# Decay products over 128 tokens instead of 64 in an attention that feeds two matrix layers

## The chip, the core and the metric

The kernel runs on one core of a Trainium2 chip. That core has a matrix engine (TensorE, PE in the profile; its weight loads are PEld), a vector engine (VectorE, DVE), a scalar engine (ScalarE, ACT), a third elementwise engine (GpSimd, POOL) and a queue that issues transfers (SyncE, SP). The metric is the device time of one execution in microseconds.

## What is computed

A recurrent attention over 4 batches, 8 heads and 768 tokens of width 48, and behind it two layers of 384 to 2048 to 384 over the 3072 tokens. Per head, token by token:

```
cur   = (u * k_t) outer v_t
y_t   = r_t @ (state + cur)
state = w_t[:, None] * state + k_t outer v_t
```

The first layer has the activation 0 below -1, h above 1 and (h+1)^2/4 between; the second has h * sigmoid(1.702 h). Weights come as 64-bit floats and are turned into 32-bit floats on the chip; every 32-bit product is made of three products of rounded parts (high by high, high by low, low by high).

## The kernel before

**Windows.** The attention is done in 24 windows of 128 tokens of one batch, 6 per batch, all 8 heads at once: 4 head pairs `m`, two heads `hh` of a pair on partitions 0 to 63 and 64 to 127. A window has two chunks `c` of 64 tokens, so 8 pieces `mc`. Inside a window the decays are products: two scans on VectorE (L423 from the right end of a piece, L425 from the left) make `rr` and `pp`, both in one buffer `pi`; k is multiplied by `rr` (L430, VectorE), r by `pp` (GpSimd). In the first seven windows (`RIP_N = 7`) r is scaled in place (L433) and ScalarE copies it into the two tiles `ra` later (L484); from the eighth on GpSimd writes the scaled r straight into `ra`, with two instructions of 64 partitions (L437). Each piece has a slot of 65 elements in `pi`, and a product starts anew in each.

**Scores and state.** The matrix engine transposes k (L464), makes the scores `sc` of each piece (L469) and the products k by v of both chunks, `kv` (L498). A tile `ra` holds scaled r in one half of the partitions and masked scores in the other (L474 copies them in under a mask, after L455 has put the u term on the diagonal). A tile `lt` holds the state in one half and v in the other, so that one matmul with K = 128 gives y (L504, `yt`). The state of the first chunk is put into `lt` by GpSimd, multiplied by the chunk's whole product `pcs` (`put`, L446); after `kv` VectorE adds it to the state (`upd`, L510) into `us`, GpSimd multiplies `us` by the second chunk's product and puts it in the second chunk's place of `lt` (L446 again), and `yt` of the second chunk follows. ScalarE squares all scaled values with a running sum (L449, L450, L486, L528): the sums decide at the end whether the numbers stayed in range.

**Layers.** The 3072 tokens go through each layer in 8 tiles of 384, in 16 steps a tile. A step `s` is: nine matmuls into `hp` (L651; two buffers while the attention runs), the low part `gl` of step s-1 (L676), nine matmuls of step s-3 into `acc` (L660, second layer L669), and the activation of step s: DVE L688, ACT L689, DVE L701, ACT L682 for the high part `gh`. A buffer of `hp` is free when L701 has read it, two steps on.

**Order.** Up to step 15 of the first tile a scheduler orders the instructions, with its own model of durations. In that part the 32 pieces of the first layer's weights are converted (DVE L638 and L642, ACT L640, POOL L644) and split (L169, L178). From step 16 on every engine's order is the order of the code. Three windows are spread over the 16 steps of a tile: a window is a generator that does one portion per slot (`attn_slot`), and 24 slots fall on 16 steps, so that windows meet the steps in three different positions, which come back in every tile. The second layer's weights are converted in the same stretch (ACT L640, L147, L148 and the vector engines).

Of the kernel before, what the change touches and what calls it, by code (L numbers as in the profile page):

```python
# [9 lines left out]
F32 = mybir.dt.float32  # L10
# [3 lines left out]
AF = mybir.ActivationFunctionType  # L14
ALU = mybir.AluOpType
# [86 lines left out]
def fast_path(st, tc, rkw_t, nat, v_l, w1, w2, u, out, x2_d, w2_d, flag_i, force):  # L102
# [79 lines left out]
    def eng_of(pat, i):  # L182
        return (nc.gpsimd, nc.vector)[pat[i % len(pat)]]
# [156 lines left out]
    with ExitStack() as sa:  # L340
# [9 lines left out]
        stu = at.tile([128, 2], F32, name="stu")  # L350
        stat = at.tile([128, NW, 4], F32, name="stat")
        rk = [at.tile([128, RKW], F32, name=f"rk{i}") for i in range(2)]
        lt = [at.tile([128, 2, MC * D + 16], F32, name=f"lt{i}") for i in range(2)]

        def slots(t, a, j):
            return t[:, a:a + WW].rearrange("p (a b) -> p a b", b=C + 1)[:, :, j]

        def consts():
            nc.gpsimd.memset(ident, 1.0)
            nc.gpsimd.affine_select(out=ident, in_=ident, pattern=[[-1, 128]], compare_op=ALU.is_equal, fill=0.0, base=0, channel_multiplier=1)  # L360
            nc.scalar.activation(out=idn, in_=ident, func=AF.Copy, scale=-1.0)
            nc.gpsimd.memset(mk_f, 1.0)
            for hh in range(2):
                p = slice(64 * hh, 64 * hh + 64)
                nc.gpsimd.affine_select(out=mk_f[p], in_=mk_f[p], pattern=[[1, C]], compare_op=ALU.is_gt, fill=0.0, base=0, channel_multiplier=-1)
            nc.vector.tensor_copy(mask, mk_f)
            nc.vector.memset(one_s, PMIN)
            nc.vector.memset(slots(one_s, 1, C), 1.0)
            nc.vector.memset(seed, PMIN)

        def prep(i):
# [20 lines left out]
        def load_v(n):  # L392
            i = n % 2
            tv = a2.tile([128, NP, 2, D], F32, tag="vn", name="vn")
            nc.sync.dma_start(out=tv, in_=nat[n, :, 2 * MC * D:].rearrange("p (m h d) -> p m h d", h=2, d=D))
            vn_t[n] = tv
            for hh in range(2):
                p = slice(64 * (1 - hh), 64 * (1 - hh) + 64)
                nc.sync.dma_start(out=lt[i][p, hh, 0:MC * D], in_=v_l[n, hh])

        tile_of = {}
        for i, (t0, n) in enumerate(TILES):
# [3 lines left out]
        def window(n):  # L406
# [10 lines left out]
            pi = a2.tile([128, 2 * WW + 1], F32, tag="pi", name="pi", bufs=PI_B)  # L417
            pp, rr = pi[:, 0:WW], pi[:, WW:]
            pcs = a2.tile([128, MC], F32, tag="pcs", name="pcs")
# [18 lines left out]
            def lt_s(t, hh, c):  # L438
                p = slice(64 * hh, 64 * hh + D)
                return t[p, hh, 0:MC * D].rearrange("p (m c d) -> p m c d", c=NC2, d=D)[:, :, c, :]  # L440

            def put(us, c):
                for hh in range(2):
                    p = slice(64 * hh, 64 * hh + D)
                    pc = pcs.rearrange("p (m c) -> p m c", c=NC2)[p, :, c:c + 1].to_broadcast([D, NP, D])
                    nc.gpsimd.tensor_tensor(out=lt_s(lt[i], hh, c), in0=us[p], in1=pc, op=ALU.mult)  # L446

            yield
            nc.scalar.activation(out=pp, in_=pp, func=AF.Square, accum_out=stat[:, n, 0:1])  # L449
            nc.scalar.activation(out=rr[:, 1:], in_=rr[:, 1:], func=AF.Square, accum_out=stat[:, n, 3:4])  # L450
            nc.vector.tensor_reduce(bb, nt[:, 0:MC * D].rearrange("p (a d) -> p a d", d=D), axis=AX.X, op=ALU.add)
            yield
            for hh in range(2):
                p = slice(64 * (1 - hh), 64 * (1 - hh) + 64)
                nc.gpsimd.affine_select(out=ra[hh][p], in_=bb[p, :, None].to_broadcast([64, MC, C]), pattern=[[0, MC], [1, C]], compare_op=ALU.is_equal, fill=0.0, base=0, channel_multiplier=-1)  # L455
            if PUT == 0 and not first:
                put(carry.pop(), 0)
            yield
            if n + 1 < NW:
                load_rkn(n + 1)  # L460
# [5 lines left out]
            for mc in range(MC):  # L466
                for hh in range(2):
                    p = slice(64 * hh, 64 * hh + D)
                    nc.tensor.matmul(out=sc[64 * (1 - hh):64 * (1 - hh) + 64, mc, :], lhsT=kt[p, mc, :], rhs=(rt[p, mc, :] if n < RIP_N else ra[hh][p, mc, :]), start=True, stop=True)  # L469
            kn_t = a2.tile([128, NP, 128], F32, tag="ktok", name="ktok", bufs=1)  # L470
            nc.scalar.activation(out=kn_t, in_=tp, func=AF.Copy)
            for hh in range(2):
# [44 lines left out]
            if not last:  # L517
                carry.append(upd(1))
# [296 lines left out]
def layout(inputs):  # L815
    r, k, v, w, u = (inputs[n] for n in "rkvwu")
    res = {}

    def tr(a):
        a = a.reshape(B, NP, 2, WPB, W, D).transpose(0, 3, 2, 5, 1, 4)  # L820
        return a.reshape(NW, 2, D, NP * W)

    wt = np.zeros((NW, 2, D, MC, C + 1), np.float32)
    wt[..., 1:] = tr(w).reshape(NW, 2, D, MC, C)
# [9 lines left out]
    res["v_l"] = nat(v)  # L834
# [29 lines left out]
```

## Time and profile before

| | us |
|---|---|
| median of 3 runs | 1037.53 |
| lowest and highest run | 1035.62, 1037.84 |
| the profiled execution | 1035.07 |
| its span, first to last instruction | 1033.3 |
| PE busy in it | 950.6 (92%) |
| DVE, ACT, POOL busy | 604.1, 517.5, 469.6 |

The page's slices show the matrix engine's busy share below 90% in the first six of 40 slices and at 90% or more in nearly all of the rest. Busy matmuls are pipelined, so a busy matrix engine is not one at its peak; what counts is where it waits.

### The profile page before, as it was taken

How to read it: one execution, taken by the hardware profiler on the slowest of the kernel's cores; microseconds unless marked ns; L12 is line 12 of the kernel's file. 1: busy time of each engine (PE TensorE's matmuls, PEld its weight loads, DVE VectorE, ACT ScalarE, POOL GpSimd, SP SyncE). 2: the span in 40 equal slices, each digit the busy share in tenths (PEclk: the TensorE clock that was granted, in tenths of full speed). 3: DMA queues.
4: the chain of work that ended last, by engine and by line, in shares of the span. 5: the costliest groups of instructions: out<-in, count | busy, mean ns of one | idle time of the engine just before them, and what ended most of it. 6: DMA issues, size and time to landing. Idle time of an engine off the chain costs nothing.

```text
span 1033.3 us, 18712 instructions
## 1 busy us (share of the span) xinstructions
PE 950.6 (92%) x6976; PEld 903.7 (87%) x6976; DVE 604.1 (58%) x1007; ACT 517.5 (50%) x1221; POOL 469.6 (45%) x481
## 2 busy tenths in 40 slices
PE   4645889999999999999999999999999999999997
PEld 2434769989888988898989999999999999999997
DVE  8999984787877777778674663323232323232321
ACT  5654554565555655546653565455555433333332
POOL 6897872676676666766662342111111111111111
PEclk8756989999999999999999999999999999999999
DMA  9763422644534545434310543232323110101000
GB/s 250 203 191 107 129 56 56 188 126 128 145 103 110 147 129 142 131 103 126 101 43 5 167 153 108 62 107 62 108 62 109 30 46 1 47 2 46 15 9 27
DMA packets 52228, 100.20 MB, mean 97 GB/s; under 512 B 8608, under 2 KB 34464, under 8 KB 52128
## 3 DMA queue, kind: packets, MB, share of 16 engines
q1 hardware_dynamic: 52128, 98.91, 33.2%
q8 instruction: 57, 0.93, 0.4%
q14 instruction: 43, 0.35, 0.1%
HBM read 81.97 MB, written 15.73 MB: 95 GB/s over the span
## 4 chain that ended last, share of the span: by engine, by line
PE 57%; DVE 17%; POOL 8%; ACT 6%; issue 6%; DMA 4%; SPq 2%; POOLq 0%; ACTq 0%; DVEq 0%
PE hp L651 27%; PE acc L669 20%; PE acc L660 8%; DVE pi L423 2%; DVE t L701 2%; ACT gh L682 2%; DVE ra L474 2%; DVE pi L425 2%; DVE gl L676 1%; DVE wt L638 1%; DMA wst<-w 1%; POOL ra L437 1%; POOL rkn L426 1%; POOL wt L644 1%; DVE wt L642 1%
## 5 line engine op out<-in xcount | busy, mean ns | idle before, releaser
L676 POOL TENSOR_TENSOR gl<-t,gh 128x384 fp32r<-128x384 f32 x128 | 132.0, 1031 | 387.7 <-ACT gh L682 386.1
L682 ACT ACTIVATE gh<-t 128x384 fp32r<-128x384 f32 x256 | 133.9, 523 | 205.5 <-DVE t L701 122.9
L712 DVE TENSOR_TENSOR t<-t,hp 128x384 f32<-128x384 f32 x128 | 70.8, 553 | 218.6 <-ACT t L707 218.1
L707 ACT ACTIVATE t<-hp 128x384 f32<-128x384 f32 x128 | 63.0, 492 | 145.8 <-PE hp L651 145.8
L660 PE MATMUL acc<-gh,whi 128*128 128x384 f32 x384 | 132.4, 350 | 0.3 <-DVE ev L252 0.3
L660 PE MATMUL acc<-gl,whi 128*128 128x384 f32 x384 | 130.2, 339 | 1.2 <-DVE gl L676 1.2
L669 PE MATMUL acc<-wlo,gh 128*128 128x384 f32 x384 | 130.2, 339 | 0.0
L669 PE MATMUL acc<-whi,gh 128*128 128x384 f32 x384 | 129.9, 338 | 0.0
L660 PE MATMUL acc<-gh,wlo 128*128 128x384 f32 x384 | 129.6, 338 | 0.0
L669 PE MATMUL acc<-whi,gl 128*128 128x384 f32 x384 | 129.3, 337 | 0.0
L651 PE MATMUL hp<-xh,whi 128*128 128x384 f32 x384 | 95.9, 359 | 24.1 <-DVE t L701 23.0
L676 DVE TENSOR_TENSOR gl<-t,gh 128x384 fp32r<-128x384 f32 x128 | 81.4, 636 | 47.0 <-ACT gh L682 44.6
L689 ACT ACTIVATE t<-t 128x384 f32<-128x384 f32 x128 | 66.3, 518 | 78.7 <-DVE t L688 76.8
L701 DVE TENSOR_TENSOR t<-t,hp 128x384 f32<-128x384 f32 x128 | 70.1, 548 | 51.9 <-ACT t L689 51.1
L644 POOL TENSOR_TENSOR wt<-wt,wb 128x384 int32<-128x384 int32 x64 | 71.7, 1121 | 62.0 <-ACT wb L640 51.1
L651 PEld LDWEIGHTS hp<-xh,whi 128*128 128x128 f32 x384 | 67.8, 193 | 33.3 <-DVE t L701 29.9
L688 DVE TENSOR_SCALAR t<-hp 128x384 f32<-128x384 f32 x128 | 70.4, 550 | 41.7 <-PE hp L651 41.6
L651 PE MATMUL hp<-xl,whi 128*128 128x384 f32 x384 | 90.2, 344 | 0.0
L651 PE MATMUL hp<-xh,wlo 128*128 128x384 f32 x384 | 89.4, 341 | 0.0
L651 PE MATMUL hp<-x2l,whi 128*128 128x384 f32 x384 | 88.8, 339 | 0.0
L651 PE MATMUL hp<-x2h,wlo 128*128 128x384 f32 x384 | 88.0, 337 | 0.0
L651 PE MATMUL hp<-x2h,whi 128*128 128x384 f32 x384 | 87.4, 335 | 0.0
(106 smaller groups left out, 1944.3 us busy)
## 6 DMA issues: line engine op xcount, KB each, us to landing
wst<-w SPq DMA_DIRECT2D x96, 384.0 KB, 3.4
rk<-rkw_t SPq DMA_DIRECT2D x48, 289.7 KB, 4.9
rkn<-nat SPq DMA_DIRECT2D x24, 384.0 KB, 4.1
w_d<-wt SPq DMA_DIRECT2D x32, 192.0 KB, 3.3
w2f<-w_d SPq DMA_DIRECT2D x32, 192.0 KB, 2.5
vn<-nat SPq DMA_DIRECT2D x24, 192.0 KB, 3.0
lt<-v_l SPq DMA_DIRECT2D x48, 96.0 KB, 3.0
x_d<-ev SPq DMA_DIRECT2D x24, 192.0 KB, 2.5
```

The source lines that it names most:

```text
L423: nc.vector.tensor_tensor_scan(out=rr[:, WW:0:-1], data0=ws[:, WW:0:-1], data1=one_s[:, WW:0:-1], initial=0.0, op0=ALU.mult, op1=ALU.max)
L644: nc.gpsimd.tensor_tensor(out=t, in0=t, in1=b, op=ALU.add)
L651: nc.tensor.matmul(out=hp[:, 0:n], lhsT=win(a, f, kk), rhs=b[:, kk, 0:n], start=(i == 0), stop=(i == 3 * KD - 1))
L660: nc.tensor.matmul(out=acc[j][:, 0:n], lhsT=wout(a, f, j * 128, 128), rhs=b[:, 0:n], start=(f == 0 and i == 0), stop=(f == KF - 1 and i == 2))
L669: nc.tensor.matmul(out=o[:, 0:DM], lhsT=a[:, j * 128:(j + 1) * 128], rhs=wout(b, f, 0, DM), start=(f == 0 and i == 0), stop=(f == KF - 1 a ...
L676: eng.tensor_tensor(out=gl[:, 0:n], in0=t[:, 0:n], in1=gh[:, 0:n].bitcast(F32), op=ALU.subtract)
L682: nc.scalar.activation(out=gh[:, 0:n], in_=t[:, 0:n], func=AF.Copy)
L688: nc.vector.tensor_scalar(t[:, 0:n], hp[:, 0:n], scalar1=-1.0, scalar2=1.0, op0=ALU.max, op1=ALU.min)
L689: nc.scalar.activation(out=t[:, 0:n], in_=t[:, 0:n], func=AF.Square, bias=0.5, scale=0.5)
L701: nc.vector.tensor_tensor(out=t[:, 0:n], in0=t[:, 0:n], in1=hp[:, 0:n], op=ALU.max)
L707: nc.scalar.activation(out=t[:, 0:n], in_=hp[:, 0:n], func=AF.Sigmoid, scale=1.702)
L712: nc.vector.tensor_tensor(out=t[:, 0:n], in0=t[:, 0:n], in1=hp[:, 0:n], op=ALU.mult)
```

## The change

The products run over a whole window of 128 tokens: 4 slots of 129 elements instead of 8 of 65. Then:

- `pcs` has 4 columns instead of 8 and is copied by ScalarE instead of VectorE.
- r is scaled in place by GpSimd in all windows (one instruction of 128 partitions); ScalarE copies it into both `ra` in all windows.
- The state of the second chunk is the sum alone: VectorE writes it straight into `lt`; GpSimd's second `put` is gone, and the addition stands ahead of the first chunk's `yt` in the code.
- The two halves of `pi` are squared by one instruction; r and k by two instead of one. Scale factors keep the squares in range.
- `lt` has slots of 64 elements instead of 48, filled by a load of 128 KB instead of 96 KB.

```diff
-WW = MC * (C + 1)
+WW = NP * (W + 1)
-PMIN = 1e-10
+PMIN = 1e-15
+DSC = 1e-5
-K_E = (1,)
-RIP_N = 7
-        lt = [at.tile([128, 2, MC * D + 16], F32, name=f"lt{i}") for i in range(2)]
+        lt = [at.tile([128, 2, MC, 64], F32, name=f"lt{i}") for i in range(2)]
...
-            nc.vector.tensor_copy(pcs, slots(rr, 1, 0))
-            eng_of(K_E, n).tensor_tensor(out=kt, in0=kt, in1=rr[:, 1:].rearrange("p (a b) -> p a b", b=C + 1)[:, :, 1:C + 1], op=ALU.mult)
-            pr = pp.rearrange("p (a b) -> p a b", b=C + 1)[:, :, 0:C]
-            if n < RIP_N:
-                nc.gpsimd.tensor_tensor(out=rt, in0=rt, in1=pr, op=ALU.mult)
-            else:
-                for hh in range(2):
-                    p = slice(64 * hh, 64 * hh + 64)
-                    nc.gpsimd.tensor_tensor(out=ra[hh][p], in0=rt[p], in1=pr[p], op=ALU.mult)
+            nc.scalar.activation(out=pcs, in_=slots(rr, 1, 0), func=AF.Copy)
+            kw = rk[i][:, NP * W:OW].rearrange("p (a b) -> p a b", b=W)
+            nc.vector.tensor_tensor(out=kw, in0=kw, in1=rr[:, 1:].rearrange("p (a b) -> p a b", b=W + 1)[:, :, 1:W + 1], op=ALU.mult)
+            rw = rk[i][:, 0:NP * W].rearrange("p (a b) -> p a b", b=W)
+            nc.gpsimd.tensor_tensor(out=rw, in0=rw, in1=pp.rearrange("p (a b) -> p a b", b=W + 1)[:, :, 0:W], op=ALU.mult)
...
-            nc.scalar.activation(out=pp, in_=pp, func=AF.Square, accum_out=stat[:, n, 0:1])
-            nc.scalar.activation(out=rr[:, 1:], in_=rr[:, 1:], func=AF.Square, accum_out=stat[:, n, 3:4])
+            sq = pi.rearrange("p (a b) -> p a b", b=WW + 1)[:, :, 0:WW]
+            nc.scalar.activation(out=sq, in_=sq, func=AF.Square, scale=DSC, accum_out=stat[:, n, 0:1])
...
-            if n < RIP_N:
-                for hh in range(2):
-                    p = slice(64 * hh, 64 * hh + 64)
-                    nc.scalar.activation(out=ra[hh][p], in_=rt[p], func=AF.Copy)
-            sq = rk[i][:, 0:OW]
-            nc.scalar.activation(out=sq, in_=sq, func=AF.Square, accum_out=stat[:, n, 1:2])
+            for hh in range(2):
+                p = slice(64 * hh, 64 * hh + 64)
+                nc.scalar.activation(out=ra[hh][p], in_=rt[p], func=AF.Copy)
+            nc.scalar.activation(out=rw, in_=rw, func=AF.Square, scale=DSC, accum_out=stat[:, n, 1:2])
+            nc.scalar.activation(out=kw, in_=kw, func=AF.Square, accum_out=stat[:, n, 3:4])
...
             def upd(c):
-                us = a2.tile([128, NP, D], F32, tag="us", name="us")
+                us = a2.tile([128, NP, D], F32, tag="us", name="us") if c else None
                 for hh in range(2):
                     p = slice(64 * hh, 64 * hh + D)
-                    nc.vector.tensor_tensor(out=us[p], in0=lt_s(lt[i], hh, c), in1=kv[c][p], op=ALU.add)
+                    nc.vector.tensor_tensor(out=us[p] if c else lt_s(hh, 1), in0=lt_s(hh, c), in1=kv[c][p], op=ALU.add)
                 return us
 
             mm_kv()
+            upd(0)
             mm_y(0)
-            put(upd(0), 1)
```

Three places show how instructions move. The first is ScalarE in the part whose order is the code's, at the thirteenth window: `gh` and `t` belong to the layer's steps, `wb` and `wj` to the conversion of the second layer's weights, `ktok` is the transposed k, `rk` the tile of r, k and w, and `ra` the right-hand side of `yt`. Before:

```order
L689 ACTIVATE t<-t 128x384
L471 ACTIVATE ktok<-tp 128x512
L682 ACTIVATE gh<-t 128x384
L640 ACTIVATE wb<-wst 128x384
L147 ACTIVATE wj,wsum<-wst 128x384
L148 ACTIVATE wj,wmin<-wj 128x384
L486 ACTIVATE rk_160,stat<-rk_160 128x1024
L689 ACTIVATE t<-t 128x384
```

The same place now:

```order
L683 ACTIVATE t<-t 128x384
L466 ACTIVATE ktok<-tp 128x512
L676 ACTIVATE gh<-t 128x384
L634 ACTIVATE wb<-wst 128x384
L146 ACTIVATE wj,wsum<-wst 128x384
L147 ACTIVATE wj,wmin<-wj 128x384
L478 ACTIVATE ra_3072<-rk_160 64x512
L478 ACTIVATE ra_3073<-rk_160 64x512
L479 ACTIVATE rk_160,stat<-rk_160 128x512
L480 ACTIVATE rk_160,stat<-rk_160 128x512
L683 ACTIVATE t<-t 128x384
```

Where one square stood there are two copies and two squares; what is ahead of them is the same. The second place is GpSimd in the same part, around the eleventh window: `lt` is the state's tile, `rkn` the products for the u term. Before:

```order
L446 TENSOR_TENSOR lt_163<-us,pcs 48x4x48 x2
L644 TENSOR_TENSOR wt<-wt,wb 128x384
L676 TENSOR_TENSOR gl<-t,gh 128x384
L446 TENSOR_TENSOR lt_163<-us,pcs 48x4x48 x2
L426 TENSOR_TENSOR rkn<-rkn 128x384
L427 TENSOR_TENSOR rkn<-rkn,u_n 128x384
L437 TENSOR_TENSOR ra_2551<-rk_160,pi 64x512
L437 TENSOR_TENSOR ra_2552<-rk_160,pi 64x512
L676 TENSOR_TENSOR gl<-t,gh 128x384
```

The same place now:

```order
L441 TENSOR_TENSOR lt_163<-us,pcs 48x4x48 x2
L638 TENSOR_TENSOR wt<-wt,wb 128x384
L670 TENSOR_TENSOR gl<-t,gh 128x384
L425 TENSOR_TENSOR rkn<-rkn 128x384
L426 TENSOR_TENSOR rkn<-rkn,u_n 128x384
L432 TENSOR_TENSOR rk_160<-rk_160,pi 128x512
L670 TENSOR_TENSOR gl<-t,gh 128x384
```

Two products of the state and one of the two products of r are gone. The third place is VectorE in the scheduled part, around the last conversion of a weight piece (`wt`): `t` and `hp` are the activation of the layer's steps, `wlo` a weight's low part. Before, the last `wt<-wst,wt`:

```order
L510 TENSOR_TENSOR us<-lt_163,kv_1340 48x192 x2
L423 SCALAR_TENSOR_TENSOR pi<-rk_161,one_s 128x520
L178 TENSOR_TENSOR wlo_0_135<-wt,whi_0_103 128x384
L701 TENSOR_TENSOR t<-t,hp 128x384
L424 RECIPROCAL seed<-pi 128x8
L430 TENSOR_TENSOR rk_161<-rk_161,pi 128x512
L701 TENSOR_TENSOR t<-t,hp 128x384
L638 TENSOR_SCALAR wt<-wst 128x384
L425 SCALAR_TENSOR_TENSOR pi<-rk_161,seed 128x520
L642 SCALAR_TENSOR_TENSOR wt<-wst,wt 128x384
```

Now:

```order
L695 TENSOR_TENSOR t<-t,hp 128x384
L682 TENSOR_SCALAR t<-hp 128x384
L670 TENSOR_TENSOR gl<-t,gh 128x384
L695 TENSOR_TENSOR t<-t,hp 128x384
L531 TENSOR_TENSOR xl<-xr,xh 128x3x128
L632 TENSOR_SCALAR wt<-wst 128x384
L682 TENSOR_SCALAR t<-hp 128x384
L177 TENSOR_TENSOR wlo_0_135<-wt,whi_0_103 128x384
L636 SCALAR_TENSOR_TENSOR wt<-wst,wt 128x384
```

The eighth window's scans stand beside the last conversion before and well ahead of it now. Up to the last conversion VectorE's order holds `t<-hp` of nine steps before and of seven now; up to the sixteenth `t<-hp` it holds the same instructions but for the eight copies of `pcs`.

## Rows read from the trace of the kernel before

**Rows 1.** Stages: us, busy us (instructions) of each engine, PE clock, DMA share, GB/s
```profile
0.00:150.00 150.00, 91.10 (x802) 71.34 (x802) 140.31 (x197) 78.87 (x176) 117.67 (x120) 0.76 0.58 159
150.00:550.00 400.00, 383.61 (x3473) 357.12 (x3473) 295.73 (x515) 225.33 (x561) 258.14 (x270) 1.00 0.41 116
```

**Rows 2.** Waits of PE, 150 to 550 us: total, times, longest
```profile
PE hp L651 <- DVE t L701: 10.7, 17, 1.2
PE yt L504 <- POOL lt L446: 3.0, 6, 0.8
PE yt L504 <- POOL lt L477: 2.3, 4, 0.7
```

**Rows 3.** PE in order of time: start, us, instructions, idle before and its releaser
```profile
386.44 0.69 PE L504 MATMUL yt<-ra,lt 128*64 128x64 f32 x16
...
395.00 0.80 PE L651 MATMUL hp<-xh,whi 128*128 128x384 f32 x3 [0.53 <-DVE t L701]
...
398.92 0.80 PE L651 MATMUL hp<-xh,whi 128*128 128x384 f32 x3 [0.49 <-DVE t L701]
...
409.31 0.69 PE L504 MATMUL yt<-ra,lt 128*64 128x64 f32 x16
...
427.74 0.80 PE L651 MATMUL hp<-xh,whi 128*128 128x384 f32 x3 [0.67 <-DVE t L701]
...
430.80 0.33 PE L504 MATMUL yt<-ra,lt 128*64 128x64 f32 x2 [0.71 <-POOL lt L477]
431.55 0.68 PE L504 MATMUL yt<-ra,lt 128*64 128x64 f32 x14 [0.42 <-POOL lt L477]
```

**Rows 4.** ACT in order of time, same stretch
```profile
386.09 1.04 ACT L486 ACTIVATE rk<-rk 128x1024 f32<-128x1024 f32 x1
...
409.31 1.05 ACT L486 ACTIVATE rk<-rk 128x1024 f32<-128x1024 f32 x1
...
422.88 0.64 ACT L449 ACTIVATE pi<-pi 128x520 f32<-128x520 f32 x1 [2.64 <-POOL ra L437]
...
432.97 1.05 ACT L486 ACTIVATE rk<-rk 128x1024 f32<-128x1024 f32 x1
```

**Rows 5.** Groups, whole run: busy us, mean ns, idle before and releasers
```profile
L446 POOL TENSOR_TENSOR lt<-us,pcs 48x192 f32<-48x192 f32 x88 | 52.7, 599 | 18.4 <-DVE us L510 11.1 <-PE yt L504 4.1
L437 POOL TENSOR_TENSOR ra<-rk,pi 64x512 f32<-64x512 f32 x34 | 45.1, 1325 | 14.8 <-DVE pi L425 13.5
L486 ACT ACTIVATE rk<-rk 128x1024 f32<-128x1024 f32 x24 | 25.1, 1044 | 0.1
L449 ACT ACTIVATE pi<-pi 128x520 f32<-128x520 f32 x24 | 15.1, 629 | 10.2 <-POOL ra L437 9.8 <-POOL rk L433 0.3
L433 POOL TENSOR_TENSOR rk<-rk,pi 128x512 f32<-128x512 f32 x7 | 9.2, 1311 | 3.1 <-issue 1.5 <-DVE pi L425 1.4
L484 ACT ACTIVATE ra<-rk 64x512 f32<-64x512 f32 x14 | 8.7, 623 | 0.8 <-POOL rk L433 0.7
L486 ACT ACTIVATION_READ_ACCUMULATOR rk<-rk 128x1 f32 x24 | 4.5, 186 | 0.0
```

**Rows 6.** DVE in order of time, same stretch as rows 3
```profile
390.30 0.36 DVE L510 TENSOR_TENSOR us<-lt,kv 48x192 f32<-48x192 f32 x1 [0.24 <-POOL lt L446]
...
396.65 1.15 DVE L429 COPY pcs<-pi 128x8 f32<-128x8 f32 x1
```

**Rows 7.** Groups of DVE, 0 to 150 us
```profile
L642 DVE SCALAR_TENSOR_TENSOR wt<-wst,wt 128x384 int32<-128x384 int32 x32 | 30.2, 947 | 0.4
...
L429 DVE COPY pcs<-pi 128x8 f32<-128x8 f32 x8 | 5.1, 632 | 0.1
```

**Rows 8.** Line L642 alone, 0 to 150 us: min/median/max ns, first and last start
```profile
L642 DVE SCALAR_TENSOR_TENSOR wt<-wst,wt x32: 525/875/2651, 8.6 to 146.9; 128x384 int32<-128x384 int32 x32
```

**Rows 9.** The last conversion (DVE) and the start of PE's seventeenth step
```profile
146.88 0.53 DVE L642 SCALAR_TENSOR_TENSOR wt<-wst,wt 128x384 int32<-128x384 int32 x1
...
171.56 0.79 PE L651 MATMUL hp<-xh,whi 128*128 128x384 f32 x3
```

More of the change, by code (lines that the diff above doesn't have):

```diff
@@ L367, in consts @@
             nc.vector.memset(one_s, PMIN)
-            nc.vector.memset(slots(one_s, 1, C), 1.0)
+            nc.vector.memset(slots(one_s, 1, W), 1.0)
             nc.vector.memset(seed, PMIN)
@@ L398, in load_v @@
                 p = slice(64 * (1 - hh), 64 * (1 - hh) + 64)
-                nc.sync.dma_start(out=lt[i][p, hh, 0:MC * D], in_=v_l[n, hh])
+                nc.sync.dma_start(out=lt[i][p, hh], in_=v_l[n, hh])
         tile_of = {}
@@ L416, in window @@
             kn = nt[:, MC * D:2 * MC * D].rearrange("p (m c d) -> p m c d", c=NC2, d=D)
-            pi = a2.tile([128, 2 * WW + 1], F32, tag="pi", name="pi", bufs=PI_B)
-            pp, rr = pi[:, 0:WW], pi[:, WW:]
-            pcs = a2.tile([128, MC], F32, tag="pcs", name="pcs")
+            pi = a2.tile([128, 2 * WW + 2], F32, tag="pi", name="pi", bufs=PI_B)
+            pp, rr = pi[:, 0:WW], pi[:, WW:2 * WW + 1]
+            pcs = a2.tile([128, NP], F32, tag="pcs", name="pcs")
             ra = [a2.tile([128, MC, C], F32, tag=f"ra{h}", name=f"ra{h}", bufs=2) for h in range(2)]
@@ L428, in window, with lt_s, put @@
             yield
-            nc.vector.tensor_copy(pcs, slots(rr, 1, 0))
-            eng_of(K_E, n).tensor_tensor(out=kt, in0=kt, in1=rr[:, 1:].rearrange("p (a b) -> p a b", b=C + 1)[:, :, 1:C + 1], op=ALU.mult)
-            pr = pp.rearrange("p (a b) -> p a b", b=C + 1)[:, :, 0:C]
-            if n < RIP_N:
-                nc.gpsimd.tensor_tensor(out=rt, in0=rt, in1=pr, op=ALU.mult)
-            else:
-                for hh in range(2):
-                    p = slice(64 * hh, 64 * hh + 64)
-                    nc.gpsimd.tensor_tensor(out=ra[hh][p], in0=rt[p], in1=pr[p], op=ALU.mult)
-            def lt_s(t, hh, c):
+            nc.scalar.activation(out=pcs, in_=slots(rr, 1, 0), func=AF.Copy)
[3 more added lines that the diff above has]
+            nc.gpsimd.tensor_tensor(out=rw, in0=rw, in1=pp.rearrange("p (a b) -> p a b", b=W + 1)[:, :, 0:W], op=ALU.mult)
+            def lt_s(hh, c):
                 p = slice(64 * hh, 64 * hh + D)
-                return t[p, hh, 0:MC * D].rearrange("p (m c d) -> p m c d", c=NC2, d=D)[:, :, c, :]
-            def put(us, c):
+                return lt[i][p, hh].rearrange("p (m c) e -> p m c e", c=NC2)[:, :, c, 0:D]
+            def put(us):
                 for hh in range(2):
                     p = slice(64 * hh, 64 * hh + D)
-                    pc = pcs.rearrange("p (m c) -> p m c", c=NC2)[p, :, c:c + 1].to_broadcast([D, NP, D])
-                    nc.gpsimd.tensor_tensor(out=lt_s(lt[i], hh, c), in0=us[p], in1=pc, op=ALU.mult)
+                    nc.gpsimd.tensor_tensor(out=lt_s(hh, 0), in0=us[p], in1=pcs[p, :, None].to_broadcast([D, NP, D]), op=ALU.mult)
             yield
-            nc.scalar.activation(out=pp, in_=pp, func=AF.Square, accum_out=stat[:, n, 0:1])
-            nc.scalar.activation(out=rr[:, 1:], in_=rr[:, 1:], func=AF.Square, accum_out=stat[:, n, 3:4])
+            sq = pi.rearrange("p (a b) -> p a b", b=WW + 1)[:, :, 0:WW]
+            nc.scalar.activation(out=sq, in_=sq, func=AF.Square, scale=DSC, accum_out=stat[:, n, 0:1])
             nc.vector.tensor_reduce(bb, nt[:, 0:MC * D].rearrange("p (a d) -> p a d", d=D), axis=AX.X, op=ALU.add)
@@ L456, in window @@
             if PUT == 0 and not first:
-                put(carry.pop(), 0)
+                put(carry.pop())
             yield
@@ L468, in window @@
                     p = slice(64 * hh, 64 * hh + D)
-                    nc.tensor.matmul(out=sc[64 * (1 - hh):64 * (1 - hh) + 64, mc, :], lhsT=kt[p, mc, :], rhs=(rt[p, mc, :] if n < RIP_N else ra[hh][p, mc, :]), start=True, stop=True)
+                    nc.tensor.matmul(out=sc[64 * (1 - hh):64 * (1 - hh) + 64, mc, :], lhsT=kt[p, mc, :], rhs=rt[p, mc, :], start=True, stop=True)
             kn_t = a2.tile([128, NP, 128], F32, tag="ktok", name="ktok", bufs=1)
@@ L490, in window @@
             if PUT == 2 and not first:
-                put(carry.pop(), 0)
+                put(carry.pop())
             yt = ps_s.tile([128, NP, W], F32, tag="s", name="yt")
@@ L503, in mm_y @@
                         mc = m * NC2 + c
-                        nc.tensor.matmul(out=yt[64 * hh:64 * hh + 64, m, c * C:(c + 1) * C], lhsT=lt[i][:, hh, mc * D:mc * D + 64], rhs=ra[hh][:, mc, :], start=True, stop=True)
+                        nc.tensor.matmul(out=yt[64 * hh:64 * hh + 64, m, c * C:(c + 1) * C], lhsT=lt[i][:, hh, mc, :], rhs=ra[hh][:, mc, :], start=True, stop=True)
             def upd(c):
-                us = a2.tile([128, NP, D], F32, tag="us", name="us")
+                us = a2.tile([128, NP, D], F32, tag="us", name="us") if c else None
                 for hh in range(2):
                     p = slice(64 * hh, 64 * hh + D)
-                    nc.vector.tensor_tensor(out=us[p], in0=lt_s(lt[i], hh, c), in1=kv[c][p], op=ALU.add)
+                    nc.vector.tensor_tensor(out=us[p] if c else lt_s(hh, 1), in0=lt_s(hh, c), in1=kv[c][p], op=ALU.add)
                 return us
             mm_kv()
+            upd(0)
             mm_y(0)
-            put(upd(0), 1)
             yield
@@ L821, in tr @@
         return a.reshape(NW, 2, D, NP * W)
-    wt = np.zeros((NW, 2, D, MC, C + 1), np.float32)
-    wt[..., 1:] = tr(w).reshape(NW, 2, D, MC, C)
+    wt = np.zeros((NW, 2, D, NP, W + 1), np.float32)
+    wt[..., 1:] = tr(w).reshape(NW, 2, D, NP, W)
     res["rkw_t"] = np.concatenate([tr(r), tr(k), wt.reshape(NW, 2, D, -1), wt[..., 0, 0:1]], axis=3)
@@ L833, in layout @@
     res["nat"] = np.concatenate([flip(r), flip(k), tok(v)], axis=2)
-    res["v_l"] = nat(v)
+    vl = np.zeros((NW, 2, C, MC, 64), np.float32)
+    vl[..., 0:D] = nat(v).reshape(NW, 2, C, MC, D)
+    res["v_l"] = vl
     def slices(wi, wo):
```

6 lines of the change are left out of this document (3 added, 3 removed).

## The prediction

> **What bounds the kernel now.** I read the stages first. Up to 150 us VectorE is busy 140.31 of 150 us and the matrix engine 91.10: there VectorE sets the pace, and the reader is to see that nearly every microsecond taken from it could come back. From 150 to 550 us the matrix engine is busy 383.61 of 400 us at full clock, so that at most 16.4 us are to be had there, and a new wait on it costs its whole length; the other engines have a quarter or more of that stretch free [rows 1]. After 550 us the attention is over and no instruction of the change is left. Second, the waits of the matrix engine in the middle stage: 10.7 us for a free `hp` buffer (VectorE's L701 is late) and 3.0 + 2.3 us of `yt` for GpSimd's work on `lt` [rows 2]. Third, one tile in order of time, 386 to 432 us, with its three windows, one in each of the three positions that come back in every tile: what stands on ScalarE and VectorE where `yt` starts [rows 3, 4, 6]. Last, durations by group [rows 5, 7].
>
> **Part by part, middle stage.** 17 windows lie in it whose r went to `ra` by GpSimd before and goes through ScalarE now: six like the first of the tile shown, six like the second, five like the third.
>
> GpSimd loses, per window, two products of the state at 599 ns and one r product (2 x 1325 before, 1311 now): 2.5 us [rows 5]. It is busy 258 of 400 us and is no bound [rows 1]; what counts is who waits for it. VectorE loses the copy of `pcs`, 1.15 us in the tile shown [rows 6]. ScalarE's copy of it is not in the trace; it lies between a read-out of one column, 186 ns, and a 64-row copy of 512 columns, 623 ns [rows 5]; I take 0.2 us, near the read-out, since it has 4 columns.
>
> ScalarE gains the two copies, 2 x 623 = 1.25 us, and one read-out; two squares of half the length for one of 1044 ns are between 0.2 and 0.4 us more; one square of `pi` instead of two saves about 2 x (629 + 186) - (1044 + 186) = 0.4 us [rows 5]. Some 1.5 us more in a window, which its free time holds. But the copies are now in the path: `yt` reads `ra`, and the copies stand in ScalarE's queue where L486 stood, behind `ktok` and, in the third position, also behind a weight's `wb` and two `wj`. So I compare the time of L486 with the start of `yt`:
>
> First position: L486 at 386.09, `yt` at 386.44 [rows 3, 4]. The second copy ends at 386.09 + 1.25 = 387.34, so `yt` is 0.9 us late. Nothing upstream is quicker: the square's place there follows work that comes out of a transfer. Six times 0.9 is +5.4.
>
> Second position: L486 and `yt` both at 409.31, so 1.25 us late as it stands. But ScalarE comes there earlier. VectorE no longer waits for GpSimd before its scans (0.24 us, and as much before the instruction ahead of it) and has no `pcs` copy (1.15) [rows 6]; the square of `pi` saves 0.4 and the `pcs` copy on ScalarE takes back 0.2: together about 1.8 us. The same 1.8 us remove the matrix engine's stalls of 0.53 and 0.49 us for `hp` ahead of it [rows 3]. Copies ready at 409.31 - 1.8 + 1.25 = 408.76; `yt` could go at 409.31 - 1.02 = 408.29: 0.47 late, 1.02 gained, net -0.55. Six times is -3.3.
>
> Third position: `yt` could have gone at 430.80 - 0.71 = 430.09 and waited for GpSimd until 431.55 [rows 3]. L486 is at 432.97, so copies as it stands are ready at 434.22. Upstream the square of `pi` at 422.88 had waited 2.64 us for GpSimd's r product [rows 4]; that is 2 x 1.325 - 1.311 = 1.34 us shorter, and the joint square gives 0.4: ready at about 432.5, and the stall of 0.67 us at 427.74 goes meanwhile. What counts is the end: 432.5 against 431.55, +0.95. Five times is +4.8. GpSimd's wait is not saved there, it ends behind a longer one.
>
> Sum: 5.4 - 3.3 + 4.8 = +6.9 us. Bounds: if the copies come in time everywhere, all waits of rows 2 go, -16.0; if ScalarE is no earlier anywhere and nothing is given back, 6 x 0.9 + 6 x 1.25 + 5 x (434.22 - 431.55) = +26.3.
>
> **First stage.** Eight copies of `pcs` leave VectorE, 8 x 632 ns = 5.1 us [rows 7]. About 14 products of the state leave GpSimd, 14 x 599 ns = 8.4 us [rows 5] of the 117.67 it is busy there [rows 1]. VectorE is slowed while GpSimd works: the 32 L642 take 525 ns at least, 947 on average and 2651 at most, 13.5 us over the least [rows 7, 8]. If that falls with GpSimd's work, 8.4/117.67 of it is 1.0 us, and as much again for other instructions: -5 to -7 us of VectorE's work.
>
> The Trainium skill ("SBUF — State Buffer", section "SBUF: two separate sides") says that VectorE and GpSimd lock a shared port pair for a whole instruction and the loser blocks. The spread of L642 agrees; by that rule GpSimd's full 8.4 us could come back, 13 us in all, and that is the faster rival below.
>
> What the matrix engine gets of it depends on the order. Up to the last conversion VectorE's order holds `t<-hp` of seven steps now and of nine before: the conversions end earlier, but two more steps of the matrix engine come behind them. A step takes 398.92 - 0.49 - 395.00 = 3.4 us [rows 3], two 6.9. Before, the seventeenth step starts 171.56 - 146.88 = 24.7 us behind the last conversion [rows 9]. VectorE's instructions up to the last conversion are fewer now by the copies and by two steps' activation (about 4 instructions of some 0.5 us): 5 to 9 us earlier, and 6.9 later behind it. The start of the seventeenth step so moves by -2 +- 5; I take -2, since the work that VectorE loses is sure and the place of the steps is not. The longer load of `lt` is hidden: transfers take 0.41 to 0.58 of the engines [rows 1], and that window's `lt` is loaded two windows ahead.
>
> **Sum.** +6.9 - 2 = +5 us. The profiled execution, span 1033.3 and time 1035.07, would become 1040; it is 2.5 us below the median of the runs, so against 1037.53 I forecast 1042.5, slower by 0.5%.
>
> **Rivals.**
> 1. Faster: VectorE's saving passes to the matrix engine. First stage -5.1 - 2 to -13, and ScalarE in the middle stage comes early enough that the copies' wait and the stalls given back cancel. For it: VectorE is busy 94% of the first stage, and in the second position most of the wait is already made up. Against: the two steps behind the last conversion, and the first position, where nothing is earlier. Typical -7: 1030.5; with the whole of rows 2 about 1017.
> 2. No change: the same terms, with +4 in the middle and -4 at the start, 1037.5. For it: both terms are of that size and of opposite sign.
> 3. Much slower: nothing is given back. ScalarE's queue is in order, and 1.5 us more in it makes every later `t` and `gh` late as well; then the waits of `hp` in rows 2 stay and the copies' waits come on top, half to all of the +26.3: 1051 to 1064. It decides as soon as the square of `pi` in the third position is not earlier than now. Against: ScalarE has 44% of that stage free there.
>
> **How the numbers follow.** Forecast 42%, its own range 1039.7 to 1048; rival 1 29%; rival 2 19%; rival 3 10%. About 0.2%, 2 us, is what a measurement of this kernel can tell from no change. Slower 0.52, same 0.19, faster 0.29. The range takes the typical case of rival 1 and the lower edge of rival 3: 1029 to 1052.
>
> **What would show it.** `yt` waits for ScalarE's copies in the third position by 2 us or more and in the first by about 1, and its waits for GpSimd are gone; the waits of `hp` for L701 fall from 10.7 to under 5; the seventeenth step starts between 165 and 175 us. I am wrong if the copies end before the matrix engine is there, or if that step starts before 164 us.

## The result and the profile after

The changed kernel takes 1050.12 us (median of 4 runs, 1047.58 to 1052.0), the kernel before 1037.68 beside it (4 runs, 1035.62 to 1037.94): ratio 1.0123, 95% interval 1.0096 to 1.0149. It is slower by 12 us, where 5 were forecast. The profiled execution took 1051.0 us, span 1049.3. The two profiled executions so lie 16.0 us apart, 3.5 more than the medians: before's was 2.5 below its median and this one 0.9 above. What is read from the two traces below carries that difference.

The two stages again (columns as in [rows 1]):

```profile
0.00:150.00 150.00, 88.95 (x827) 70.94 (x828) 135.66 (x192) 82.60 (x190) 105.04 (x110) 0.81 0.64 168
150.00:550.00 400.00, 375.20 (x3290) 352.11 (x3289) 274.11 (x479) 234.12 (x581) 206.31 (x206) 0.97 0.42 115
```

In the first stage VectorE and GpSimd have less to do, as forecast. In the middle stage every engine but ScalarE does less in the same 400 us, and the matrix engine's granted clock (its mean share of full speed), 1.00 before, is 0.97. The prediction had not looked for that last figure.

Waits of the matrix engine, 150 to 550 us (total, times, longest), against [rows 2]:

```profile
PE yt L498 <- ACT ra L478: 9.7, 3, 3.6
PE yt L498 <- issue: 7.0, 22, 0.8
PE yt L498 <- POOL wt L638: 4.2, 2, 2.1
PE hp L645 <- DVE t L695: 2.9, 3, 1.0
```

The waits for `lt` are gone and those of `hp` fell from 10.7 to 2.9. In their place `yt` waits. Three long ones are put down to ScalarE's copies, two to `wt` of GpSimd and 22 short ones to issue. But `yt` doesn't read `wt`, and a releaser is inferred. The rows below show what these are: the first two `yt` start 0.1 us behind the end of the first copy, the other fourteen 0.1 us behind the second. So it is at every `yt` of the stage that waits more than 0.1 us, whatever releaser is named.

The tile shown in [rows 3], again in order of time (start, us, instructions, idle before and its releaser):

```profile
394.91 0.30 PE L498 MATMUL yt<-ra,lt 128*64 128x64 f32 x2 [0.28 <-issue]
395.56 0.65 PE L498 MATMUL yt<-ra,lt 128*64 128x64 f32 x14 [0.35 <-issue]
...
417.18 0.30 PE L498 MATMUL yt<-ra,lt 128*64 128x64 f32 x2 [0.22 <-issue]
417.83 0.65 PE L498 MATMUL yt<-ra,lt 128*64 128x64 f32 x14 [0.35 <-issue]
...
420.10 0.69 PE L645 MATMUL hp<-xh,whi 128*128 128x384 f32 x3
...
436.96 0.57 PE L492 MATMUL kv<-vn,ktok 64*48 64x48 f32 x32
440.58 0.44 PE L498 MATMUL yt<-ra,lt 128*64 128x64 f32 x2 [3.05 <-ACT ra L478]
441.23 1.09 PE L498 MATMUL yt<-ra,lt 128*64 128x64 f32 x14 [0.21 <-issue]
442.25 0.69 PE L654 MATMUL acc<-gh,whi 128*128 128x384 f32 x1
...
445.30 1.16 PE L645 MATMUL hp<-xh,whi 128*128 128x384 f32 x3
...
449.72 0.80 PE L645 MATMUL hp<-xh,whi 128*128 128x384 f32 x3
```

In the first and second position the wait splits in two short ones. In the third it is 3.05 and 0.21 us, and what comes behind it is slow: fourteen `yt` take 1.09 us (0.68 in [rows 3]) and nine `acc` take from 442.25 to 445.30, 3.05 us. ScalarE in the third position (in the first, the two copies start at 394.20):

```profile
429.96 1.07 ACT L445 ACTIVATE pi<-pi 128x1032 f32<-128x1032 f32 x1 [1.35 <-POOL rk L432]
...
437.81 0.52 ACT L676 ACTIVATE gh<-t 128x384 fp32r<-128x384 f32 x1 [1.72 <-DVE t L695]
438.24 0.54 ACT L634 ACTIVATE wb<-wst 128x384 int32<-128x384 uint32 x1
...
439.35 0.52 ACT L147 ACTIVATE wj<-wj 128x384 f32<-128x384 f32 x1
...
439.87 1.26 ACT L478 ACTIVATE ra<-rk 64x512 f32<-64x512 f32 x2
```

The copies stand behind `gh`, `wb` and two `wj`, and end at 441.13. And the granted clock, the third number from the end (the stretch up to the end of the wait, and the stretch behind it):

```profile
418.00:440.50 22.50, 19.53 (x188) 18.47 (x185) 16.76 (x30) 14.74 (x39) 14.60 (x14) 0.98 0.46 122
440.50:447.00 6.50, 6.21 (x32) 5.97 (x33) 0.56 (x1) 2.90 (x7) 2.34 (x3) 0.54 0.63 178
```

Behind the stall TensorE gets 0.54 of its full clock: nearly all of those 6.5 us run at the lower of its two levels, 1.2 GHz in place of 2.4. The same length behind the other four long waits (0.74 means about half of the stretch at the lower level):

```profile
231.00:237.50 6.50, 5.86 (x37) 5.61 (x38) 0.71 (x2) 3.20 (x8) 2.79 (x3) 0.74 0.76 182
371.00:377.50 6.50, 5.91 (x37) 5.66 (x38) 0.75 (x2) 3.18 (x8) 2.76 (x3) 0.74 0.75 183
300.50:307.00 6.50, 5.83 (x31) 5.59 (x32) 0.55 (x1) 3.26 (x8) 2.71 (x3) 0.54 0.71 184
512.50:519.00 6.50, 5.88 (x32) 5.63 (x33) 0.55 (x1) 3.21 (x8) 2.78 (x3) 0.56 0.51 121
```

PE counts as busy there. Its clock and the longer matmuls tell that it is slow, not its busy share.

**Where the 17 us lie.** The start of each step's first `hp` matmul, in both traces, gives how far the changed kernel lags, step by step. Counted from the seventeenth step, where it is 1.6 us ahead, up to the end of attention, and put down to the position in which it grows, with the forecast beside it:

```
position   windows   forecast   lag gained in the middle stage
first         6        +5.4        +4.65
second        6        -3.3        -3.24
third         5        +4.8       +16.93
sum                    +6.9       +18.3
```

Two terms of three came out to within 0.8 us. The third is 12 us too small.

### The profile page after: what moved, and what is told of

It reads as the page before. It is cut to its first block, busy times and chain, and to the rows that moved or that the text cites. A ratio compares the mean times of both kernels' runs of the same rounds, so it can differ in the third digit from the quotient of the medians.

```text
span 1049.3 us, 18649 instructions
## 1 busy us (share of the span) xinstructions
PE 956.6 (91%) x6976; PEld 913.9 (87%) x6976; DVE 586.5 (56%) x983; ACT 541.1 (52%) x1279; POOL 412.4 (39%) x416
## 4 chain that ended last, share of the span: by engine, by line
PE 73%; DVE 13%; issue 5%; ACT 4%; DMA 2%; POOL 1%; SPq 1%; DVEq 0%; ACTq 0%; POOLq 0%
PE hp L645 34%; PE acc L663 19%; PE acc L654 15%; PE yt L498 2%; DVE pi L422 2%; DVE ra L469 2%; PE sc L464 2%; DMA rk<-rkw_t 1%; DVE t L695 1%; DVE pi L424 1%; DVE wt L632 1%; DVE wt L636 1%; ACT gh L676 1%; ACT ra L478 1%; PE tp L459 1%
## 5 line engine op out<-in xcount | busy, mean ns | idle before, releaser
L654 PE MATMUL acc<-gh,whi 128*128 128x384 f32 x384 | 135.0, 356 | 0.2 <-DVE ev L251 0.2
```

What stands on the lines that cost most here:

```text
L654: nc.tensor.matmul(out=acc[j][:, 0:n], lhsT=wout(a, f, j * 128, 128), rhs=b[:, 0:n], start=(f == 0 and i == 0), stop=(f == KF - 1 and i == 2))
```

## The experiments

Theory A: the place of the copies in ScalarE's queue costs the time, mostly in the third position. Theory C, beside it: a good part of that is the lower clock behind the stall. Rivals: the other parts of the change cost (B); ScalarE is overloaded wherever the copies stand (B of the second run, E); the slow matmuls have another cause (D). Times are medians; ratios are to the kernel before, run beside it, with 95% intervals. The runs were made in three groups (e1 to e4, e5 to e8, e9 to e11), and the kernel before took 1037.05, 1036.0 and 1037.12 us in them. So differences between groups, and to the changed kernel, are good to about 1 us. Line numbers shift by a few from kernel to kernel.

```
run                  us        ratio to before
e1_direct          1025.73   0.9891 (0.9873 to 0.9909)
e2_early           1026.96   0.9902 (0.9882 to 0.9922)
e3_before_copies   1061.05   1.0224 (1.0201 to 1.0247)
e4_fill            1047.58   1.0093 (1.0067 to 1.0118)
e5_gap             1042.87   1.0058 (1.0036 to 1.0079)
e6_direct_put2     1032.44   0.9959 (0.9940 to 0.9978)
e7_direct_pcs      1025.52   0.9891 (0.9869 to 0.9913)
e8_fill_sized      1043.67   1.0067 (1.0045 to 1.0089)
e9_early_third     1035.00   0.9981 (0.9971 to 0.9991)
e10_early_others   1043.26   1.0061 (1.0044 to 1.0078)
e11_direct_onesq   1023.31   0.9871 (0.9855 to 0.9888)
```

**e1_direct: the copies undone.** From the eighth window on:

```
+            if n < 7:
+                nc.gpsimd.tensor_tensor(out=rw, in0=rw, in1=pr, op=ALU.mult)
+            else:
+                for hh in range(2):
+                    p = slice(64 * hh, 64 * hh + 64)
+                    nc.gpsimd.tensor_tensor(out=ra[hh][p].rearrange(...), in0=rw[p], in1=pr[p], op=ALU.mult)
...
+            if n < 7:
                 ra copies on ScalarE
```

> The changed kernel, but from the eighth window on GpSimd writes r times the decay straight into ra (two products of 64 partitions, as before the change), and the score product reads ra; ScalarE's two copies are gone there. Theory A (the copies in ScalarE's queue are what the change costs: yt waits for them, about 3 us in each of five third positions, 0.9 us in six first ones, and a slower matrix clock behind the long waits): the time falls below before's, since the rest of the change (the hp waits that go, 1.6 us of the first stage) stays; 1026 to 1038 us, no yt wait for ScalarE left, granted clock of the middle stage back to 1.00. Rival B (the loss is in the other parts, the wider lt, the two squares, the moved copy of pcs): 1045 us or more.

1025.73 us, 24 below the changed kernel and 11 below before, and 0.3 below the range that I had given; the middle stage's clock is 1.00. Theory A holds, B falls: the other parts of the change gain time.

**e2_early: the same copies, one portion earlier.**

```
+            if n >= 7:
+                for hh in range(2):
+                    p = slice(64 * hh, 64 * hh + 64)
+                    nc.scalar.activation(out=ra[hh][p], in_=rt[p], func=AF.Copy)
             sq = pi.rearrange(...)
...
+            if n < 7:
                 ra copies at their old place
```

> The changed kernel, but from the eighth window on ScalarE's two copies of r stand one portion earlier: behind GpSimd's product of r and ahead of the square of pi, so ahead of ktok, wb and the two wj in ScalarE's queue; nothing is left out. Theory A (place in the queue, not the work of the copies, costs the time): yt no longer waits for the copies; 1028 to 1038 us, middle clock 1.00. Rival B (ScalarE's additional 1.25 us a window make t and gh late wherever the copies stand): 1045 to 1055 us, with hp or acc waiting for ScalarE or VectorE instead.

1026.96 us, 1.0 below the range, with every instruction of the change still there. Waits of the matrix engine, 150 to 550 us:

```profile
PE hp L650 <- DVE t L700: 7.7, 11, 1.2
PE yt L503 <- POOL lt L441: 2.3, 6, 0.7
PE yt L503 <- DVE t L700: 1.6, 2, 0.8
```

No wait for the copies is left; `hp` and `lt` take back some of it. ScalarE does the same work in every window: the place cost 23 us. Against e1, which does without these copies, 1.2 us are left.

**e3_before_copies: that part alone, in the kernel before.**

```
-RIP_N = 7
+RIP_N = NW
```

> The kernel before with one part of the change alone: r is scaled in place and copied by ScalarE in all 24 windows, not in the first seven only. Theory A: the whole loss comes from this part; five long waits in the third position, six of 0.9 us in the first, the second with no gain to offset it; 1050 to 1062 us. Rival B (other parts cost): within 5 us of before, 1033 to 1043 us.

1061.05 us: 24 us slower than before, as far as e1 is faster than the changed kernel. By position the lag grows by 4.9, 4.5 and 14.8 us: without the rest of the change the second position has nothing to set against its wait, and the stage's `hp` waits are 8.9 us instead of 2.9. The five long waits are there, 2.1 to 3.5 us, but only four of them were followed by the lower clock (last section).

**e4_fill and e8_fill_sized: the stall filled.** Matmuls whose result is overwritten, between `kv` and `yt`, in the five third positions:

```
             mm_kv()
             upd(0)
+            if n >= 9 and n % 3 == 0:
+                for _ in range(16):
+                    nc.tensor.matmul(out=yt.rearrange("p a b -> p (a b)")[:, 0:TN], lhsT=whi[0][0][:, 0:128], rhs=whi[0][0], start=True, stop=True)
```

(e8: `range(10 if n in (9, 15) else 15)`.)

> The changed kernel with 16 idle matmuls of 128x384 (at 0.177 us each 2.8 us of matrix work whose result is overwritten) between kv and yt in the five third positions, where the matrix engine stands still for 3 to 4 us and shows about half of the full clock behind it. Theory C (about 2 us of each of these places is the lower clock behind the stall): with the stall filled the clock stays at 1.00 there, the steps behind it take 3.4 us again, and the kernel gets faster by 5 to 11 us although it does more work, 1039 to 1046 us. Rival D (the slow steps have another cause): the time stays or grows by up to 3 us, 1049 to 1054 us.

1047.58 us, outside what I expected by 1.6 us. The clock of the middle stage is 1.00 to two places and the nine `acc` take 1.7 us again, but 16 matmuls are longer than the two shorter waits, and at 486 to 491 us a new place with short waits, put down to `ktok` and `lt`, and slow matmuls behind them (clock 0.74) cost some 2 us. So the number was fitted to the waits:

> As the run with 16 filling matmuls, but their number follows the wait that the trace of the changed kernel shows: 10 (1.8 us) in the first and third of the five third positions (waits of 2.1 us), 15 (2.7 us) in the others (3.1 to 3.6 us). Theory C (the lower clock behind the stall is itself 1 to 2 us of each place): the nine acc matmuls behind yt take 1.7 us again, not 3.05, and the five places give 8 to 11 us back, 1039 to 1044 us. Rival D: 1047 us or more, the places give back less than 4 us.

1043.67 us, 6.5 below the changed kernel (5.8 by the ratios to the kernel before), though it does some 12 us more of matrix work (65 matmuls, 15 of them in 2.87 us). The place of the tile shown, and the clock of the same stretch:

```profile
434.44 2.87 PE L511 MATMUL yt<-whi 128*128 128x384 f32 x15
437.53 0.30 PE L498 MATMUL yt<-ra,lt 128*64 128x64 f32 x2 [0.22 <-issue]
438.18 0.65 PE L498 MATMUL yt<-ra,lt 128*64 128x64 f32 x14 [0.35 <-POOL gl L673]
438.76 0.44 PE L657 MATMUL acc<-gh,whi 128*128 128x384 f32 x1
...
440.44 0.69 PE L648 MATMUL hp<-xh,whi 128*128 128x384 f32 x3
```

```profile
437.50:444.00 6.50, 6.12 (x53) 5.73 (x55) 2.29 (x6) 3.38 (x8) 2.32 (x3) 1.00 0.65 177
```

`yt` comes no earlier, since it still waits for the copies, but 0.65 and 1.68 us stand where 1.09 and 3.05 stood. By position the third one's lag falls from 16.93 to 6.3 us, by 10.6; 1.8 of that may only make good what the second position lost in this run. So 9 to 10.6 us of the loss went with the clock, not with the wait. Theory C holds, D falls. As a whole the run gains less, since the first position lost 1.0 and the second those 1.8. The 1.8 arise at 209 us, where `yt` waited 0.95 and 0.35 us for the copies and the clock fell for the nine `acc` behind it, which take 3.05 us again (last section).

**e5_gap: `kv` and `yt` one slot later.**

```
-            yield from idle(GAPS[1])
+            yield from idle(GAPS[1] + (n >= 7))
```

> The changed kernel, but from the eighth window on kv and yt of a window come one slot later in the program (one more empty portion between the copies and them); the copies stay where they are in ScalarE's queue, nothing is left out. Theory A (the copies are late against yt, by about 3 us in the third position and 0.9 in the first): a slot is 2 to 4 us of matrix work, so the waits for the copies go or fall under 1 us and the time comes to 1026 to 1036 us. Rival E (the copies are a bottleneck of ScalarE, which falls behind in every window): the waits only move, 1045 us or more.

1042.87 us, between the two. The long waits for the copies are gone (ten of 0.4 us or less are left). But a later `yt` also moves `upd` and with it VectorE's queue, and others come:

```profile
PE hp L645 <- DVE t L695: 14.5, 8, 2.9
PE acc L654 <- ACT ev L253: 2.6, 2, 1.7
```

Neither theory foresaw that price on VectorE, so the time alone doesn't decide between A and E. What speaks for A is that one slot more between the copies and `yt` ends the long waits, as the earlier copies of e2 do.

**e9_early_third and e10_early_others: by position.** The copies moved as in e2, in one set of windows alone:

```
+            if n >= 9 and n % 3 == 0:        # e10: if n >= 7 and n % 3:
                 ra copies, ahead of the square of pi
```

> The changed kernel with the copies one portion earlier in the five third positions only. If the third position carries most of the loss (steps of the matrix engine there were 2.6 to 5.1 us later than before, 17 us in all, and about 19 us against the kernel with no copies): 15 to 20 us faster than the changed kernel, 1030 to 1035 us, and the granted clock of the middle stage 1.00. If the positions share it evenly (5 of 17 windows, 7 us): 1041 to 1045 us.

> The changed kernel with the copies one portion earlier in the first and second positions only, the third as it is. By the same account what is left there is 6 x 0.9 us in the first and as much again in the second: 5 to 10 us faster than the changed kernel, 1040 to 1045 us, with the third position's waits of 2 to 3.6 us and the lower clock behind them still there. If the positions share it evenly: 1031 to 1036 us.

1035.00 us, 15.1 less, and 1043.26, 6.9 less: 22.0 together, against e2's 23.2. In e10 the long waits stay, in rows that name ScalarE three times and `wt` twice, as in the changed kernel:

```profile
PE yt L503 <- ACT ra L483: 9.5, 3, 3.4
...
PE yt L503 <- POOL wt L643: 4.1, 2, 2.1
```

Five windows of 17 carry over two thirds of what the earlier copies win back.

**e6_direct_put2 and e7_direct_pcs: what the rest is worth.** Both from e1, from the eighth window on. e6 lets the second chunk's state take its tile and two GpSimd products again, e7 gives the copy of `pcs` back to VectorE:

```
+            us0 = upd(0)
+            nc.gpsimd.tensor_tensor(out=lt_s(hh, 1), in0=us0[p], in1=<ones>, op=ALU.mult)   # e6, for both halves
...
-                nc.scalar.activation(out=pcs, in_=slots(rr, 1, 0), func=AF.Copy)
+                nc.vector.tensor_copy(pcs, slots(rr, 1, 0))                                 # e7
```

> The kernel of the first run (GpSimd writes ra directly, 1025.7 us) with one part of the change undone from the eighth window on: the second chunk's state goes through a tile and a second pair of GpSimd products (by one) again. Measures what the state as an addition alone is worth in the middle stage. My account of before (GpSimd is a quarter to a half idle there, yt waited 3.0 + 2.3 us for its work on lt): 2 to 6 us slower, 1028 to 1032 us, with yt waiting for GpSimd's lt. Rival: nothing (within 1.5 us), the gain is VectorE's.

> The kernel of the first run with another part undone from the eighth window on: VectorE copies pcs again, in place of ScalarE. Measures what taking that copy off VectorE is worth in the middle stage. My account (hp stalls of 0.53 and 0.49 us a tile in the second position come back, since VectorE is 0.6 to 1.15 us later there): 4 to 8 us slower, 1030 to 1034 us, with hp waiting 8 us or more for VectorE against 5.2. Rival: under 2 us, if the scans without the wait for GpSimd are what ended the stalls.

e6: 1032.44 us, 6.7 more than e1 and 0.4 above the range. e7: 1025.52, no different, as its rival said. By the lag against the kernel before, e1 gains 7.2 us in the middle stage and e6 0.2. So the addition alone is worth all that the rest of the change gains there, and VectorE's copy nothing. But the mechanism I had expected of e6 is not the one that shows. `yt` waits for `lt` as in e1 (2.8 and 0.8 us against 2.8 and 0.9); what doubles is the wait of `hp`, 10.2 us against 5.2. VectorE, ahead of its scans, e6:

```profile
321.02 0.34 DVE L511 TENSOR_TENSOR us<-lt,kv 48x192 f32<-48x192 f32 x1 [0.39 <-POOL lt L519]
321.61 0.36 DVE L511 TENSOR_TENSOR us<-lt,kv 48x192 f32<-48x192 f32 x1 [0.24 <-POOL lt L519]
322.00 1.76 DVE L422 TENSOR_TENSOR_SCAN pi<-rk,one_s 128x516 f32<-128x516 f32 x1
```

and e1:

```profile
319.29 0.73 DVE L511 TENSOR_TENSOR us<-lt,kv 48x192 f32<-48x192 f32 x2
320.05 1.23 DVE L422 TENSOR_TENSOR_SCAN pi<-rk,one_s 128x516 f32<-128x516 f32 x1
```

The addition for the next window waits for GpSimd's products (3.2 us in all in the stage), and the scan behind it took 1.76 us instead of 1.23; over the 16 scans of this line in the stage the mean is 1518 ns instead of 1352. Both stand ahead of VectorE's `t`, for which `hp` waits. How much each of them costs wasn't measured apart.

**e11_direct_onesq: e1 with one square over r and k**, and a clearing of the statistics tile that it needs.

```
+                both = rk[i][:, 0:OW]
+                nc.scalar.activation(out=both, in_=both, func=AF.Square, accum_out=stat[:, n, 1:2])
```

> The kernel of the first run, with one square over r and k from the eighth window on in place of two of half the length. ScalarE is 43% idle in the middle stage; nothing of its waits is late there once the copies are gone: within 1.5 us of that kernel, 1024 to 1027 us. Rival: 2 to 4 us faster, if the 0.2 to 0.4 us of each window were still on the path.

1023.31 us, the fastest, 2.4 below e1 and so in the rival's range. But of the middle stage it changes 0.7 us; the seventeenth step starts at 167.5 us in place of 170.0. The clearing also changes the order of the first stage, whose steps start elsewhere, so it isn't shown that the square is the reason.

## Why the prediction was right in sign and too small

**What came as forecast.** The costs of the instructions: a copy into `ra` 621 ns (forecast 623), the copy of `pcs` 202 (200), the two squares 0.4 us more than one (0.2 to 0.4). The first position: +4.65 us, where +5.4 was worked out from L486's start and 1.25 us. The second: -3.24 against -3.3. The `hp` waits fell under 5 us. `yt` no longer waits for `lt`. And the third position's `yt` waits for the copies by over 2 us.

**The step that failed** is the third position, "the end counts: 432.5 against 431.55, +0.95". To compare, take the lag at the step behind the second position away. The kernel before:

```profile
411.62 0.69 PE L651 MATMUL hp<-xh,whi 128*128 128x384 f32 x3
...
432.16 0.44 PE L660 MATMUL acc<-gh,whi 128*128 128x384 f32 x1
...
433.85 0.68 PE L651 MATMUL hp<-xh,whi 128*128 128x384 f32 x3
...
437.72 0.79 PE L651 MATMUL hp<-xh,whi 128*128 128x384 f32 x3
```

The first and the last of these steps start at 420.10 and 449.72 now: 8.48 us of lag, then 12.00. The copies' end at 441.13 is 432.65 in the time of the kernel before; 432.5 was forecast. The fourteen `yt` start at 441.23 - 8.48 = 432.75, 1.20 behind 431.55; 0.95 was forecast. So the queue was read correctly, pi's square too: it starts at 429.96 - 8.48 = 421.48, 1.4 us earlier than 422.88 (forecast 1.34). But the lag grows by 12.00 - 8.48 = 3.5 us, not 1.2: the other 2.3 are 0.41 in `yt` (1.09 - 0.68), 1.36 in the nine `acc` (3.05 against 433.85 - 432.16 = 1.69) and the rest in the `hp` behind them, all at the lower clock. The prediction netted the wait against one of before, end against end, and so lost sight of its length: PE stood still about 3.3 us (0.71 and 0.42 in [rows 3]), and it did not price what a longer standstill does to the clock. In all five places the clock fell; times the length, (0.26 + 0.46 + 0.26 + 0.46 + 0.44) x 6.5 = 12.2 us of full-clock time were not granted, a bound from above for what the clock cost there. e8 got 9 to 10.6 back, and the forecast was short by 12.1. With the clock kept, as in e8, the third position's lag is 6.3 where 4.8 was forecast.

**The cause of the gain was misnamed.** I put the 1.8 us by which VectorE and ScalarE come earlier in the second position down to the `pcs` copy above all (1.15). e7 says that this copy is worth nothing there; e6 says that GpSimd's two products are worth 6.7 us, with the waits and the slower scan on VectorE as the likely way. The sum was right and its parts were not: that it came out at -3.24 is in part luck.

**The range.** The forecast's own range, 1039.7 to 1048, missed 1050.1. The stated one, up to 1052, holds it only because it took in the lower edge of rival 3, whose mechanism didn't occur. That is luck too.

**The first stage.** The seventeenth step starts 1.6 us earlier, -2 forecast. Seven profiled kernels with that program order up to there (the changed one, e2, e4, e5, e8, e9, e10) start it between 169.7 and 172.6 us, 170.8 on average; before, one execution, 171.56. The run e3, whose order up to 150 us is that of the kernel before but for GpSimd's last product there, starts it at 174.69. So the term is small, and its size isn't shown. Its two parts came as argued: the last conversion starts at 140.28 in place of 146.88, 6.6 us earlier (forecast 5 to 9), and 29.7 us lie between it and the seventeenth step in place of 24.7, 5.0 more (forecast 6.9). The 32 conversions (L636, L642 in [rows 7]) take 28.9 us in place of 30.2:

```profile
L636 DVE SCALAR_TENSOR_TENSOR wt<-wst,wt 128x384 int32<-128x384 int32 x32 | 28.9, 916 | 0.3
```

1.3 back (forecast 1.0), though in e1 they take 30.6, so this group alone is no sure measure. All of VectorE's instructions ahead of its sixteenth `t<-hp`, without the copies of `pcs`, take 144.7 us in place of 146.5: 1.8 back, where 2 were forecast. The rule on the shared port pair, in the Trainium skill ("SBUF — State Buffer", "SBUF: two separate sides"), had been priced at up to 8.4 us; that was not seen.

**The rivals.** Rival 3 named nearly the time, 1051, but not the way: pi's square was earlier and the stalls were given back. Rival 1's saving was there, under the copies: without them the kernel takes 1025.73 (e1), between its 1030.5 and 1017. Rival 2's two terms did not cancel.

The Trainium skill ("TensorE: Matmul & The Clock Gate", section "What's actually happening") says that the matrix array's rate follows how busy the engine has lately been. The rows agree: 1.00 in the middle stage of the kernel before, 0.54 to 0.74 behind the five stalls, 1.00 with these stalls filled. The prediction should have weighed it.

## What to carry to other kernels

Work that moves onto an in-order queue is priced by what stands ahead of it where it is issued, not by its length: the same two copies cost 23 us in one place and hardly anything a portion earlier. A wait on the matrix engine is priced by its whole length, also where it takes the place of a shorter one, since the matmuls behind it may run at the lower clock. And where a change has several parts, time each alone: here one part's loss of 24 us hid another's gain of 11.

## What was not expected of the hardware

In the changed kernel, waits of PE of 2.1 us were followed by 6.5 us at 0.74 and those of 3.1 to 3.6 us by 0.54 to 0.56. In the kernel before the longest was 1.2 [rows 2], and the stage ran at 1.00. Read alone, these rows make the wait's length look like the rule. The other runs show that it isn't. The same length of 6.5 us behind a wait of 2.09 us in e3, of 2.06 and of 3.09 us in e10, of 1.76 us in e5, and of 0.95 and 0.35 us in e8:

```profile
237.00:243.50 6.50, 6.07 (x51) 5.67 (x53) 2.20 (x6) 3.25 (x6) 3.56 (x5) 1.00 0.72 177
```

```profile
230.00:236.50 6.50, 6.06 (x30) 5.82 (x31) 0.55 (x1) 3.03 (x8) 2.62 (x3) 0.51 0.72 181
299.70:306.20 6.50, 6.11 (x37) 5.96 (x38) 0.78 (x2) 2.86 (x7) 2.30 (x3) 0.74 0.69 177
```

```profile
288.10:294.60 6.50, 6.41 (x63) 6.19 (x63) 4.45 (x9) 5.64 (x14) 3.92 (x6) 1.00 0.04 9
```

```profile
208.50:215.00 6.50, 6.42 (x50) 6.02 (x51) 4.57 (x9) 4.28 (x12) 1.78 (x2) 0.74 0.50 101
```

So a wait of 2.1 us kept the full clock in one place and lost it in another, and two short waits close together lost it too (0.95 and 0.35 us in e8; the changed kernel waits 0.80 and 0.35 us at the same place and keeps 1.00). Which wait it will be, and how long the clock stays low, can't be told from these runs.

Matmuls of no use, put into the five stalls, kept 1.00 there and made the kernel 6.5 us faster. The scan of 128x516 took 1.23 us in e1's row and 1.76 in e6's; why was not tried.
